# One core, two attention blocks: the fallback path moved to another DMA queue, the branch flag read earlier, the last columns in quarters

## The chip, the cores and the metric

The kernel runs on one core of a Trainium2 chip. The metric is the device time of one execution in microseconds (us). Executions of the same kernel here scatter by about 1 us in 350, so what follows leans on two things: times taken in rounds with the kernel before on the same chip, and the trace, which resolves single instructions to some nanoseconds.

## The reference, cut to what matters

Two independent problems A and B of the same shape, each a grouped-query attention block with cached K and V and an output projection; their results are placed side by side in the last axis.

```python
B, Sq, D = 16, 32, 1024;  Hq, Hkv, Sk, Dh = 32, 4, 512, 128      # all bf16
q = (x @ wq).reshape(B, Sq, Hq, Dh).transpose(0, 2, 1, 3)
scores = einsum("bhqd,bhkd->bhqk", q, repeat(k_cache, 8)) * Dh ** -0.5
o = einsum("bhqk,bhkd->bhqd", softmax(scores), repeat(v_cache, 8))
a = o.transpose(0, 2, 1, 3).reshape(B, Sq, Hq * Dh) @ wo          # and the same for B
return concatenate([a, b], axis=-1)
```

## The kernel before

The kernel has a fast path, which shifts the exponent by a constant instead of by each row's maximum, and a general path, which is slow and safe. The fast path counts how many row sums lie in a safe range; at the end every engine reads that count (the flag) and branches: if the count is full, it skips the general path. With these inputs the general path never runs. It is in the program all the same.

The parts that matter, with cuts:

```python
def general_path(tc, problems, out_flat):            # never executed here
    ...
            nc.sync.dma_start(out=x_sb[:], in_=x_v)                       # also wq, wo, outputs: all SyncE
    ...
                nc.sync.dma_start_transpose(out=kT[:], in_=k_rows[r0:r0 + HKV * SK, :])
    ...

            def f_units(pr, tt, n0, width, eng):     # output projection, one matmul per yield
                ps = psum.tile([P, NW], FP32, name="f_ps", tag="proj")
                for h in range(HQ):
                    nc.tensor.matmul(ps[:, 0:width], lhsT=oT[pr, tt][:, h, :], ...)
                    if h == HQ - 1:
                        o_sb = outp.tile([P, NW], BF16, name="o_sb")
                        if eng is nc.scalar:
                            nc.scalar.copy(out=o_sb[:, 0:width], in_=ps[:, 0:width])
                        else:
                            nc.vector.tensor_copy(out=o_sb[:, 0:width], in_=ps[:, 0:width])
                        eng.dma_start(out=out_flat[...], in_=o_sb[:, 0:width])
                    yield

            def stream():                            # the filler matmuls, in order
                ...
                for tts in ((0, 1), (2,)):
                    for nh in range(NH):
                        for tt in tts:
                            yield from f_units(1, tt, nh * NW, NW, nc.gpsimd)
                yield from f_units(1, TT - 1, 0, NW, nc.gpsimd)
                yield from f_units(1, TT - 1, NW, QW, nc.sync)            # 256 columns
                yield from f_units(1, TT - 1, NW + QW, QW, nc.scalar)     # the last 256
    ...
            nc.tensor.matmul(ok_ps[:], lhsT=cnt[:], rhs=one_col[:], start=True, stop=True)
            nc.vector.tensor_copy(out=ok_i[:], in_=ok_ps[:])
            run(units, 1 << 20)                      # all the output units that are left

    fast_path(ok_i)
    total = 2 * 2 * NG * QW
    ok = nc.values_load(ok_i[0:1, 0:1], ...)         # on every engine
    with tc.If(ok < total, preferred_fallthrough_block=True, label="general"):
        general_path(tc, problems, out_flat)
```

DMAs of the hardware queues (issued by SyncE and ScalarE) signal eight semaphores in turn, a ring, so the semaphore that the last output signals depends on how many such DMAs came before it (in the traces: numbers 101 and 103 to 109 in turn; the last output signals the first of them, 101, in the kernel before and the last, 109, in the changed one). Where the branch is skipped, each engine still has to bring the semaphores that the skipped code would have raised to the values that later code expects; for those of DMAs, the engine that would have issued them does it (in the trace of the kernel before, SyncE's eight events on the branch's line each wait for one semaphore and raise it).

Of the kernel before, what the change touches and what calls it, by code (L numbers as in the profile page):

```python
# [8 lines left out]
BF16 = mybir.dt.bfloat16  # L9
# [7 lines left out]
P = 128  # L17
HQ = 32
DH = 128
HKV = 4  # L20
# [10 lines left out]
def general_path(tc, problems, out_flat):  # L31

    nc = tc.nc
# [4 lines left out]
    KC = SK // P  # L38
# [4 lines left out]
    with ExitStack() as ctx:  # L43
# [10 lines left out]
        for x, k_cache, v_cache, wq, wo, col_off in problems:  # L54
            x_v = x.flatten_outer_dims().rearrange("(t p) d -> p t d", p=P)
            x_sb = wpool.tile([P, TT, D], BF16, name="g_x", tag="g_w")
            nc.sync.dma_start(out=x_sb[:], in_=x_v)
            xT = big.tile([P, DC, NTOK], BF16, name="g_xT")
            for tt in range(TT):
                ps = psum.tile([P, DC, P], BF16, name="g_xT_ps", tag="g_t", bufs=2)  # L60
# [6 lines left out]
            wq_v = wq.rearrange("(c p) n -> p c n", p=P)  # L67
            for c in range(HQ // WH):
                wq_sb = wpool.tile([P, DC, WH * DH], BF16, name="g_wq", tag="g_w")
                nc.sync.dma_start(  # L70
                    out=wq_sb[:], in_=wq_v[:, :, c * WH * DH:(c + 1) * WH * DH]
                )
                for hl in range(WH):
                    q_ps = psum.tile([P, NTOK], FP32, name="g_q_ps", tag="g_p", bufs=2)
                    for dc in range(DC):
                        nc.tensor.matmul(
                            q_ps[:],
                            lhsT=wq_sb[:, dc, hl * DH:(hl + 1) * DH],
                            rhs=xT[:, dc, :],
                            start=(dc == 0),  # L80
                            stop=(dc == DC - 1),
                        )
                    nc.scalar.mul(
                        out=qT[:, :, c * WH + hl, :],
                        in_=q_ps[:].rearrange("p (b s) -> p b s", s=SQ),
                        mul=SCALE,
                    )
            oT = big.tile([P, HQ, NTOK], BF16, name="g_oT")
            k_rows = k_cache.rearrange("b g k d -> (b g k) d")
            for b in range(B):  # L90
                kT = kvpool.tile([P, HKV, SK], BF16, name="g_kT")
                r0 = b * HKV * SK
                nc.sync.dma_start_transpose(out=kT[:], in_=k_rows[r0:r0 + HKV * SK, :])
                v_sb = kvpool.tile([P, HKV, KC, DH], BF16, name="g_v")
                nc.sync.dma_start(
                    out=v_sb[:], in_=v_cache[b].rearrange("g (c p) d -> p g c d", p=P)
                )
                for g in range(HKV):
                    s_ps = psum.tile([P, 2, SK], FP32, name="g_s_ps", tag="g_s")
                    for half in range(2):  # L100
                        h0 = g * REP + half * HALF
                        nc.tensor.matmul(
                            s_ps[:, half, :],
                            lhsT=qT[:, b, h0:h0 + HALF, :].rearrange("p h s -> p (h s)"),
                            rhs=kT[:, g, :],
                            start=True,
                            stop=True,
                        )
                    nmx = work.tile([P, 2], FP32, name="g_nmx")
                    nc.vector.tensor_reduce(  # L110
                        out=nmx[:], in_=s_ps[:], axis=AX.X, op=ALU.max, negate=True
                    )
                    p_sb = work.tile([P, 2, SK], BF16, name="g_p_sb")
                    rs = work.tile([P, 2], FP32, name="g_rs")
                    rr = work.tile([P, 2], FP32, name="g_rr")
                    for half in range(2):
                        nc.scalar.activation(
                            out=p_sb[:, half, :], in_=s_ps[:, half, :], func=ACTF.Exp,
                            bias=nmx[:, half:half + 1], scale=1.0,
                            accum_out=rs[:, half:half + 1],  # L120
                        )
                    nc.vector.reciprocal(out=rr[:], in_=rs[:])
                    for half in range(2):
                        nc.vector.tensor_scalar_mul(
                            out=p_sb[:, half, :], in0=p_sb[:, half, :],
                            scalar1=rr[:, half:half + 1],
                        )
                    pT_ps = psum.tile([P, KC, 2 * P], BF16, name="g_pT_ps", tag="g_t", bufs=2)
                    for half in range(2):
                        for kc in range(KC):  # L130
                            nc.tensor.transpose(
                                pT_ps[:, kc, half * P:(half + 1) * P],
                                p_sb[:, half, kc * P:(kc + 1) * P],
                                ident[:],
                            )
                    pT = work.tile([P, KC, 2 * P], BF16, name="g_pT")
                    nc.vector.tensor_copy(out=pT[:], in_=pT_ps[:])
                    o_ps = psum.tile([P, 2 * P], FP32, name="g_o_ps", tag="g_p", bufs=2)
                    for kc in range(KC):
                        nc.tensor.matmul(  # L140
                            o_ps[:],
                            lhsT=v_sb[:, g, kc, :],
                            rhs=pT[:, kc, :],
                            start=(kc == 0),
                            stop=(kc == KC - 1),
                        )
                    nc.scalar.copy(
                        out=oT[:, g * REP:(g + 1) * REP, b * SQ:(b + 1) * SQ],
                        in_=o_ps[:].rearrange("p (h s) -> p h s", s=SQ),
                    )  # L150
            wo_v = wo.rearrange("(h p) n -> p h n", p=P)
            for oc in range(NOUT // OCW):
                wo_sb = wpool.tile([P, HQ, OCW], BF16, name="g_wo", tag="g_w")
                nc.sync.dma_start(out=wo_sb[:], in_=wo_v[:, :, oc * OCW:(oc + 1) * OCW])
                for tt in range(TT):
                    f_ps = psum.tile([P, OCW], FP32, name="g_f_ps", tag="g_p", bufs=2)
                    for h in range(HQ):
                        nc.tensor.matmul(
                            f_ps[:],
                            lhsT=oT[:, h, tt * P:(tt + 1) * P],  # L160
                            rhs=wo_sb[:, h, :],
                            start=(h == 0),
                            stop=(h == HQ - 1),
                        )
                    o_sb = work.tile([P, OCW], BF16, name="g_o_sb")
                    nc.vector.tensor_copy(out=o_sb[:], in_=f_ps[:])
                    c0 = col_off + oc * OCW
                    nc.sync.dma_start(
                        out=out_flat[tt * P:(tt + 1) * P, c0:c0 + OCW], in_=o_sb[:]
                    )  # L170

# [2 lines left out]
def kernel(  # L174
# [35 lines left out]
    def fast_path(ok_i):  # L210
        with ExitStack() as fctx:
# [139 lines left out]
            def run(units, n):  # L351
                for _ in range(n):
                    next(units, None)
# [190 lines left out]
            def stream():  # L544
                for h in range(2, HQ):
                    yield from q_units(0, h)
                for h in range(HQ):
                    yield from q_units(1, h)
                for nh in range(NH):
                    for tt in range(TT):  # L550
                        yield from f_units(0, tt, nh * NW, NW, nc.gpsimd)
                for tts in ((0, 1), (2,)):
                    for nh in range(NH):
                        for tt in tts:
                            yield from f_units(1, tt, nh * NW, NW, nc.gpsimd)
                yield from f_units(1, TT - 1, 0, NW, nc.gpsimd)
                yield from f_units(1, TT - 1, NW, QW, nc.sync)
                yield from f_units(1, TT - 1, NW + QW, QW, nc.scalar)

            units = stream()  # L560
            run(units, (REP - 2) * DC + 4)
# [56 lines left out]
            for k, (lim, op) in enumerate(((1.0 / SUM_HI, ALU.is_ge), (1.0 / SUM_LO, ALU.is_le))):  # L618
# [7 lines left out]
            ok_ps = psum.tile([1, 1], FP32, name="ok_ps", tag="s")  # L626
            nc.tensor.matmul(ok_ps[:], lhsT=cnt[:], rhs=one_col[:], start=True, stop=True)  # L627
            nc.vector.tensor_copy(out=ok_i[:], in_=ok_ps[:])
            run(units, 1 << 20)

    flag = ctx.enter_context(tc.tile_pool(name="flag", bufs=1))
    ok_i = flag.tile([1, 1], I32, name="ok_i")
    fast_path(ok_i)
    total = 2 * 2 * NG * QW
    ok = nc.values_load(ok_i[0:1, 0:1], min_val=0, max_val=total,
                        skip_runtime_bounds_check_because="only compared")
    with tc.If(ok < total, preferred_fallthrough_block=True, label="general"):
        general_path(tc, problems, out_flat)

# [29 lines left out]
```

## Time and profile before

| | before |
|---|---|
| time, median of the first three runs | 350.49 us (349.77 to 350.71) |
| span of the profiled run | 348.6 us |
| TensorE busy | 342.2 us, 98% |
| last ScalarE cast to the end of the span | 4.27 us |

From the page of the kernel before, its first line, the busy line and the chain that ended last:

```profile
span 348.6 us, 5527 instructions
...
PE 342.2 (98%) x2217; PEld 221.2 (63%) x2217; DVE 282.6 (81%) x420; ACT 180.4 (52%) x197; POOL 8.9 (3%) x21
...
PE 96%; DMA 2%; SPq 1%; DVE 1%; issue 0%; ACT 0%
```

The windows view of the kernel before gives, for each stretch of the span, its length and then the busy time of each engine in it, the granted clock (PEclk), the DMA share and the DMA rate:

```profile
core 0: us, PE busy (x) PEld busy (x) DVE busy (x) ACT busy (x) POOL busy (x), PEclk, DMA share, GB/s
...
11.00:179.00 168.00, 168.00 (x1072) 107.89 (x1069) 138.03 (x197) 108.53 (x130) 0.00 (x0) 1.00 1.06 256
179.00:327.00 148.00, 147.93 (x956) 96.50 (x955) 136.10 (x201) 67.90 (x61) 7.15 (x13) 1.00 0.70 173
327.00:345.00 18.00, 17.34 (x115) 10.79 (x113) 5.16 (x11) 0.37 (x1) 1.08 (x2) 1.00 0.06 21
345.00:349.00 4.00, 0.00 (x0) 0.00 (x0) 0.00 (x0) 0.00 (x0) 0.00 (x0) 1.00 0.06 18
```

TensorE is full from 11 to 327 us, so in that stretch nothing is to be won by moving other work. Only the end is open. From the timeline of the kernel before (start, duration, engine, line, what it does):

```profile
344.07 0.27 PE L331 MATMUL f_ps<-wo_sb,oT 128*128 128x256 bf16 x1
344.38 0.37 ACT L341 CAST o_sb<-f_ps 128x256 bf16<-128x256 f32 x1 [22.13 <-PE f_ps L331]
344.78 0.38 ACTq L345 DMA_DIRECT2D out_dram<-o_sb  x1
```

The list of DMA issues says how long that last output takes to land, from its issue to the last update of its semaphore (the last figure, in us):

```profile
out_dram<-o_sb ACTq DMA_DIRECT2D x1, 64.0 KB, 1.6
```

What comes after it does not count as busy, but the profile lists it by source line. L637 is the branch, L664 the end of the kernel. A row gives the sequencer, the instruction, how many, the durations in ns, and when the first and the last of them began:

```profile
L637 SPq EVENT_SEMAPHORE  x8: 17/17/17, 346.4 to 347.0; - x8
...
L637 PEldq COMPARE_BRANCH  x1: 376/376/376, 342.8 to 342.8; - x1
...
L637 ACTq COMPARE_BRANCH  x1: 79/79/79, 345.8 to 345.8; - x1
```

```profile
L664 SPq EVENT_SEMAPHORE  x14: 17/28/28, 347.0 to 348.6; - x14
...
L664 SPq DRAIN  x3: 7/7/13, 347.8 to 348.1; - x3
```

So when the last output has landed (346.42), SyncE goes through 8 events of the skipped branch, then the 12 of the end list, and only at 347.77 executes its first DRAIN, from which the closing barriers begin: 1.35 us for 20 events.

### The profile page before, as it was taken

How to read it: one execution, taken by the hardware profiler on the slowest of the kernel's cores; microseconds unless marked ns; L12 is line 12 of the kernel's file. 1: busy time of each engine (PE TensorE's matmuls, PEld its weight loads, DVE VectorE, ACT ScalarE, POOL GpSimd, SP SyncE). 2: the span in 40 equal slices, each digit the busy share in tenths (PEclk: the TensorE clock that was granted, in tenths of full speed). 3: DMA queues.
4: the chain of work that ended last, by engine and by line, in shares of the span. 5: the costliest groups of instructions: out<-in, count | busy, mean ns of one | idle time of the engine just before them, and what ended most of it. 6: DMA issues, size and time to landing. Idle time of an engine off the chain costs nothing.

```text
span 348.6 us, 5527 instructions
## 1 busy us (share of the span) xinstructions
PE 342.2 (98%) x2217; PEld 221.2 (63%) x2217; DVE 282.6 (81%) x420; ACT 180.4 (52%) x197; POOL 8.9 (3%) x21
## 2 busy tenths in 40 slices
PE   7999999999999999999999999999999999999995
PEld 4556666666666666666666666666666666666554
DVE  2118988888988889898889989999999999899710
ACT  3347667666666766666654454454455445445000
POOL 0000000000000000000000000000000000000010
PEclk9999999999999999999999999999999999999999
DMA  7999999899997899999999459995589995400000
GB/s 224 240 302 333 168 253 270 241 276 256 270 253 197 172 249 222 311 267 268 279 316 222 115 124 270 349 212 121 137 259 263 252 227 102 120 18 0 15 32 20
DMA packets 125069, 71.70 MB, mean 206 GB/s; under 512 B 73616, under 2 KB 124048, under 8 KB 125040
## 3 DMA queue, kind: packets, MB, share of 16 engines
q1 hardware_dynamic: 124176, 69.29, 81.7%
q0 software_dynamic: 720, 1.97, 1.7%
q8 instruction: 18, 0.29, 0.3%
q14 instruction: 11, 0.09, 0.1%
q10 hardware_dynamic: 144, 0.07, 0.1%
HBM read 51.38 MB, written 2.10 MB: 153 GB/s over the span
## 4 chain that ended last, share of the span: by engine, by line
PE 96%; DMA 2%; SPq 1%; DVE 1%; issue 0%; ACT 0%
PE f_ps L331 32%; PE q_ps L312 31%; PE ob L431 16%; PE s_ps L371 16%; DMA x_sb<-in_A_x_dram 2%; PE q_ps L516 1%; SPq L468 0%; DVE parts L390 0%; PE sums L407 0%; SPq L471 0%; DVE o_sb L343 0%; PE xT_ps L506 0%; ACT o_sb L341 0%; DVE cs L399 0%; PE ok_ps L627 0%
## 5 line engine op out<-in xcount | busy, mean ns | idle before, releaser
L379 ACT ACTIVATE p_sb<-s_ps,shift 128x1024 bf16<-128x1024 f32 x128 | 142.5, 1113 | 113.1 <-PE s_ps L371 100.4
L390 DVE TRANSPOSE_TENSOR_REDUCE parts<-p_sb 128x32 f32<-128x1024 bf16 x128 | 158.2, 1236 | 22.1 <-ACT p_sb L379 21.6
L331 PE MATMUL f_ps<-wo_sb,oT 128*128 128x512 bf16 (+1 forms) x544 | 133.3, 367 | 0.0
L312 PE MATMUL q_ps<-xT,wq_sb 128*128 128x512 bf16 x496 | 129.6, 380 | 0.0
L371 PE MATMUL s_ps<-qT,kT 128*128 128x256 bf16 x512 | 76.8, 273 | 0.0
L431 PE MATMUL ob<-p_sb,v_sb 128*128 128x256 bf16 x512 | 76.8, 273 | 0.0
L331 PEld LDWEIGHTS <-oT 128*128 128x128 bf16 x544 | 53.0, 98 | 33.8
L312 PEld LDWEIGHTS <-wq_sb 128*128 128x128 bf16 x496 | 48.4, 98 | 34.7 <-DMA wq_sb<-in_A_wq_dram 0.3
L371 PEld LDWEIGHTS <-kT 128*128 128x128 bf16 x512 | 56.9, 113 | 20.9
L431 PEld LDWEIGHTS <-v_sb 128*128 128x128 bf16 x512 | 50.1, 98 | 19.8 <-DVE oT L453 0.2
L453 DVE TENSOR_TENSOR oT<-r,ob 128x512 bf16<-128x512 f32 x64 | 43.9, 685 | 12.8 <-PE ob L431 9.4
L418 DVE STREAM_TRANSPOSE r<-rall 128x512 f32<-128x512 f32 x64 | 45.5, 711 | 2.2
L320 ACT CAST qT<-q_ps 128x512 bf16<-128x512 f32 x62 | 36.1, 583 | 21.3 <-PE q_ps L312 19.2
L407 PE MATMUL sums<-cs,fold 128*128 128x16 f32 x64 | 22.9, 357 | 0.1
L343 DVE CAST o_sb<-f_ps 128x512 bf16<-128x512 f32 (+1 forms) x16 | 10.8, 673 | 10.8 <-PE f_ps L331 10.0
L399 DVE TENSOR_REDUCE cs<-parts 128x16 fp32r<-128x64 f32 x64 | 16.8, 262 | 2.2
L407 PEld LDWEIGHTS sums<-cs,fold 128*128 128x128 f32 x64 | 12.1, 190 | 8.3 <-DVE cs L399 0.9
L345 POOL DMA_DIRECT2D out_dram<-o_sb x15 | 8.2, 549 | 329.3 <-DVE o_sb L343 298.6
L416 DVE RECIPROCAL rall<-sums 128x16 f32<-128x16 f32 x64 | 14.1, 220 | 0.0
L341 ACT CAST o_sb<-f_ps 128x256 bf16<-128x256 f32 x1 | 0.4, 372 | 22.1 <-PE f_ps L331 22.1
L509 DVE COPY xT<-xT_ps 128x512 bf16<-128x512 bf16 x4 | 1.7, 424 | 5.6 <-PE xT_ps L506 5.6
L509 ACT COPY xT<-xT_ps 128x512 bf16<-128x512 bf16 x4 | 2.3, 585 | 5.7 <-PE xT_ps L506 5.7
(27 smaller groups left out, 24.1 us busy)
## 6 DMA issues: line engine op xcount, KB each, us to landing
v_sb<-in_A_v_cache_dram SPq DMA_DIRECT2D x16, 512.0 KB, 5.0
wq_sb<-in_B_wq_dram SPq DMA_DIRECT2D x8, 1024.0 KB, 6.5
wo_sb<-in_A_wo_dram SPq DMA_DIRECT2D x8, 1024.0 KB, 7.6
v_sb<-in_B_v_cache_dram SPq DMA_DIRECT2D x16, 512.0 KB, 4.5
wo_sb<-in_B_wo_dram SPq DMA_DIRECT2D x8, 1024.0 KB, 8.8
wq_sb<-in_A_wq_dram SPq DMA_DIRECT2D x7, 1024.0 KB, 7.4
out_dram<-o_sb POOLq DMA_DIRECT2D x15, 128.0 KB, 3.6
x_sb<-in_A_x_dram SPq DMA_DIRECT2D x4, 256.0 KB, 3.9
```

What stands on the lines that cost most here:

```text
L312: nc.tensor.matmul(ps[:], lhsT=w[:, dc, (h % 4) * DH:(h % 4 + 1) * DH], rhs=xT[pr][:, dc, :], start=(dc == 0), stop=(dc == DC - 1),)
L320: nc.scalar.copy(out=qT[pr, g][:, :, hl, :], in_=ps[:].rearrange("p (b s) -> p b s", s=SQ),)
L331: nc.tensor.matmul(ps[:, 0:width], lhsT=oT[pr, tt][:, h, :], rhs=wo_tiles[pr, nh, h // REP][:, h % REP, off:off + width], start=(h == 0), ...
L371: nc.tensor.matmul(s_ps[:, c, :], lhsT=kT[:, i % GRP, c, :], rhs=qT[pr, g][:, b, :, :].rearrange("p h s -> p (h s)"), start=True, stop=True,)
L379: nc.scalar.activation(out=p_sb[:], in_=s_ps[:], func=ACTF.Exp, bias=shift[:], scale=SCALE)
L390: nc.vector.tensor_reduce(out=parts[j][:, q, :, :].rearrange("p c h -> p (c h)"), in_=st[i]["p"][:].rearrange("p c (h s) -> p (c h) s", s=SQ),
L399: nc.vector.tensor_reduce(out=cs[:], in_=parts.pop(j)[:].rearrange("p q c h -> p q h c"), axis=AX.X, op=ALU.add,)
L407: nc.tensor.matmul(sums[:], lhsT=fold[:].rearrange("p r s -> p (r s)"), rhs=cs[:].rearrange("p q h -> p (q h)"), start=True, stop=True,)
L416: nc.vector.reciprocal(out=rall[:, j, :], in_=pair.pop(j)[:])
L418: nc.vector.transpose(out=r[:].rearrange("p n s -> p (n s)"), in_=rall[:, j, :].unsqueeze(2).to_broadcast([P, 2 * REP, SQ]),)
L431: nc.tensor.matmul(ob[j][:, q, :], lhsT=v_sb[:, i % GRP, c, :], rhs=st[i]["p"][:, c, :], start=(c == 0), stop=(c == KC - 1),)
L453: nc.vector.tensor_tensor(out=out, in0=rcp.pop(j)[:].rearrange("p (q h) s -> p q h s", h=REP), in1=ob.pop(j)[:].rearrange("p q (h s) -> p ...
```

## The change

Four edits: the general path issues all its DMAs from GpSimd and transposes K on TensorE; six output DMAs of problem B move from GpSimd to SyncE; the last 256 columns become two units of 128; the flag is loaded 24 matmuls into the output matmuls that are left, rather than after all of them. The intent is a shorter end. Cut to its core:

```diff
-            nc.sync.dma_start(out=x_sb[:], in_=x_v)
+            nc.gpsimd.dma_start(out=x_sb[:], in_=x_v)
 ... (the same for wq, wo, V and the outputs of the general path)
-                nc.sync.dma_start_transpose(out=kT[:], in_=k_rows[r0:r0 + HKV * SK, :])
+                k_sb = kvpool.tile([P, HKV, KC, DH], BF16, name="g_k")
+                nc.gpsimd.dma_start(out=k_sb[:], in_=k_cache[b].rearrange(...))
+ ... (four TensorE transposes and one copy for each g)
-                            yield from f_units(1, tt, nh * NW, NW, nc.gpsimd)
+                            yield from f_units(1, tt, nh * NW, NW, nc.sync)
                 yield from f_units(1, TT - 1, 0, NW, nc.gpsimd)
                 yield from f_units(1, TT - 1, NW, QW, nc.sync)
-                yield from f_units(1, TT - 1, NW + QW, QW, nc.scalar)
+                yield from f_units(1, TT - 1, NW + QW, P, nc.sync)
+                yield from f_units(1, TT - 1, NW + QW + P, P, nc.scalar)
 ...
+            run(units, 24)
+            ok = nc.values_load(ok_i[0:1, 0:1], ...)
             run(units, 1 << 20)
```

More of the change, by code (lines that the diff above doesn't have):

```diff
@@ L69, in general_path @@
                 wq_sb = wpool.tile([P, DC, WH * DH], BF16, name="g_wq", tag="g_w")
-                nc.sync.dma_start(
+                nc.gpsimd.dma_start(
                     out=wq_sb[:], in_=wq_v[:, :, c * WH * DH:(c + 1) * WH * DH]
@@ L88, in general_path @@
             oT = big.tile([P, HQ, NTOK], BF16, name="g_oT")
-            k_rows = k_cache.rearrange("b g k d -> (b g k) d")
             for b in range(B):
-                kT = kvpool.tile([P, HKV, SK], BF16, name="g_kT")
-                r0 = b * HKV * SK
-                nc.sync.dma_start_transpose(out=kT[:], in_=k_rows[r0:r0 + HKV * SK, :])
+                k_sb = kvpool.tile([P, HKV, KC, DH], BF16, name="g_k")
+                nc.gpsimd.dma_start(
+                    out=k_sb[:], in_=k_cache[b].rearrange("g (c p) d -> p g c d", p=P)
+                )
                 v_sb = kvpool.tile([P, HKV, KC, DH], BF16, name="g_v")
-                nc.sync.dma_start(
+                nc.gpsimd.dma_start(
                     out=v_sb[:], in_=v_cache[b].rearrange("g (c p) d -> p g c d", p=P)
                 )
+                kT = kvpool.tile([P, HKV, SK], BF16, name="g_kT")
+                for g in range(HKV):
+                    kT_ps = psum.tile([P, KC, P], BF16, name="g_kT_ps", tag="g_t", bufs=2)
+                    for kc in range(KC):
+                        nc.tensor.transpose(kT_ps[:, kc, :], k_sb[:, g, kc, :], ident[:])
+                    nc.vector.tensor_copy(
+                        out=kT[:, g, :], in_=kT_ps[:].rearrange("p c k -> p (c k)")
+                    )
                 for g in range(HKV):
@@ L153, in general_path @@
                 wo_sb = wpool.tile([P, HQ, OCW], BF16, name="g_wo", tag="g_w")
-                nc.sync.dma_start(out=wo_sb[:], in_=wo_v[:, :, oc * OCW:(oc + 1) * OCW])
+                nc.gpsimd.dma_start(out=wo_sb[:], in_=wo_v[:, :, oc * OCW:(oc + 1) * OCW])
                 for tt in range(TT):
@@ L167, in general_path @@
                     c0 = col_off + oc * OCW
-                    nc.sync.dma_start(
+                    nc.gpsimd.dma_start(
                         out=out_flat[tt * P:(tt + 1) * P, c0:c0 + OCW], in_=o_sb[:]
@@ L628, in fast_path @@
             nc.vector.tensor_copy(out=ok_i[:], in_=ok_ps[:])
+            run(units, 24)
+            ok = nc.values_load(ok_i[0:1, 0:1], min_val=0, max_val=total,
+                                skip_runtime_bounds_check_because="only compared")
             run(units, 1 << 20)
+            return ok
     flag = ctx.enter_context(tc.tile_pool(name="flag", bufs=1))
     ok_i = flag.tile([1, 1], I32, name="ok_i")
-    fast_path(ok_i)
     total = 2 * 2 * NG * QW
-    ok = nc.values_load(ok_i[0:1, 0:1], min_val=0, max_val=total,
-                        skip_runtime_bounds_check_because="only compared")
+    ok = fast_path(ok_i)
     with tc.If(ok < total, preferred_fallthrough_block=True, label="general"):
```

## The prediction

> **What bounds the kernel now.** TensorE. The page gives PE 342.2 of 348.6 us; the chain that ended last is 96% PE. In the windows view PE is busy 168.00 of 168 us from 11 to 179 us and 147.93 of 148 from 179 to 327, at full granted clock. So only the tail after the last matmul (about 344.34 us) is open: 4.3 us.
>
> **The tail (timeline; sequencer rows of the branch's line and the last line).** Last matmul, ScalarE cast 344.38 (0.37 us), ScalarE issues the last output at 344.78, which lands after 1.6 us, at 346.42, when SyncE's first semaphore event runs. Then SyncE alone executes 8 events of the skipped branch (346.4 to 347.0: it raises each of its DMA semaphores, because the general path uses them) and 12 end-of-kernel events (to 347.7), one every 0.066 us. The first drain is at 347.77, the closing barriers 0.88 us more.
>
> **The change.**
> 1. General path on GpSimd's queue. Never executed, but the skipped branch no longer has semaphores of SyncE to raise: those 8 events vanish. GpSimd's new waits are on transfers long landed. The last output's semaphore now also comes last in SyncE's end list (built program). From landing to the first drain: 1.35 us becomes one wait, 0.07. Saves 1.3 us, all on the critical path.
> 2. Flag loaded early. A load costs 0.48 to 0.54 us per sequencer. In before, ScalarE's runs in the shadow of the final landing: its drain is at 346.3, just before 346.42. TensorE's load begins with 17 matmuls still to start, so it runs ahead of the array; 0.5 us mid-stream is covered (the Trainium skill, "TensorE: Matmul & The Clock Gate", Architectural detail, gives a 64-deep queue; 17 pairs are 34 instructions, so this trace shows at least that). Worth about 0 alone.
> 3. Quarters: 32 matmuls of 256 columns, 109.3 ns apart, become 64 of 128. The trace's own 128-column matmuls with weight loads start 56 ns apart (the same page, Back-to-back issue gap, says about 81 sustained; the trace is used): 3.58 against 3.50 us, +0.08, minus 0.05 for the shorter last matmul. The ScalarE cast shrinks from 0.37 to about 0.27 (estimate from 512 columns 0.58, 256 columns 0.37). Net -0.07 us; the 32 KB landing stays near 1.6.
> 4. Six B outputs move from GpSimd to SyncE. Their casts are ready while SyncE waits for buffers, so K/V loads slip by at most an issue (0.4 us) against microseconds of slack. 0 us.
>
> Sum: -1.3 to -1.4 us. Predicted 349.1 us, 80% range 348.4 to 350.0. Chances: faster by over 2%: 1%; within 2%: 98%; slower: 1%.
>
> **What would show it.** Step 1: SyncE's branch line has no semaphore events; landing to first drain about 0.1 us. Step 2: no gap of PE near 337 us. Step 3: last-unit matmuls 56 ns apart, last cast about 0.27 us at about 344.4. Step 4: windows from 179 to 327 us still full PE. Span 347.2 to 347.4.
>
> **What would make it wrong.** TensorE's queue running dry after its flag load (up to +0.6 us); 128-column pairs at 66 to 81 ns (+0.7 to +1.7 us); narrow 256-byte rows landing more slowly; ScalarE or GpSimd arriving after the landing (the jump over the now larger branch; ScalarE took 0.42 us after its compare); a SyncE output wait holding back a V load; scatter (0.9 us between three runs before).

## The result, and the profile after

Beside the kernel before, the changed kernel took 349.5 us (median of 4, 349.34 to 349.55) against 350.51 (4 runs). Ratios here are the mean time of one kernel's runs over that of the other's of the same rounds, with the first run of each set (the profiled one) left out, so not quite the ratio of the quoted medians: 0.9976, 95% interval 0.9961 to 0.9990, or -0.84 us. A second set of rounds with the unaltered changed kernel (after_again, below) gave 0.9966 (0.9953 to 0.9980), or -1.19 us.

The page of the changed kernel:

```profile
span 347.7 us, 5593 instructions
...
PE 342.7 (99%) x2249; PEld 221.7 (64%) x2249; DVE 283.0 (81%) x421; ACT 180.5 (52%) x197; POOL 5.7 (2%) x15
...
PE 96%; DMA 2%; SPq 1%; DVE 1%; issue 0%; ACT 0%
```

Its windows: the middle is as full as it was, so no output on SyncE's queue held back a load that TensorE waited for.

```profile
11.00:179.00 168.00, 168.00 (x1072) 107.89 (x1070) 138.06 (x197) 108.64 (x130) 0.00 (x0) 1.00 1.04 257
179.00:327.00 148.00, 147.94 (x955) 96.41 (x954) 136.22 (x201) 67.96 (x61) 4.46 (x8) 1.00 0.67 172
```

Its timeline at the end, and the landing in its list of issues:

```profile
344.56 0.27 ACT L349 CAST o_sb<-f_ps 128x128 bf16<-128x128 f32 x1 [22.21 <-PE f_ps L339]
344.86 0.38 ACTq L353 DMA_DIRECT2D out_dram<-o_sb  x1
```

```profile
out_dram<-o_sb ACTq DMA_DIRECT2D x1, 32.0 KB, 1.9
```

The branch (L648) and the end of the kernel (L675). SyncE has no event at the branch any more, and its end list starts at 343.7, before the last output is even issued:

```profile
L648 PEldq COMPARE_BRANCH  x1: 397/397/397, 343.4 to 343.4; - x1
L648 SPq COMPARE_BRANCH  x1: 68/68/68, 343.5 to 343.5; - x1
```

```profile
L675 SPq EVENT_SEMAPHORE  x14: 17/28/28, 343.7 to 347.7; - x14
...
L675 SPq DRAIN  x3: 7/7/13, 346.8 to 347.1; - x3
```

The difference of the two spans (-0.93 us) adds up from the two traces:

| from the trace, us | before | after | difference |
|---|---|---|---|
| start to first exponential (start-up) | 23.19 | 23.30 | +0.11 |
| first to last exponential | 297.94 | 297.94 | 0.00 |
| last exponential to last cast (TensorE's last units) | 23.25 | 23.33 | +0.08 |
| last cast to issue of the last output | 0.40 | 0.30 | -0.10 |
| issue to landing, as SyncE sees it | 1.64 | 1.90 | **+0.26** |
| landing to SyncE's first drain | 1.35 (20 events) | 0.07 (1 event) | -1.29 |
| drain to the end of the span | 0.88 | 0.90 | +0.02 |

The second row, 297.93 or 297.94 us in all fourteen traces, is the whole pipelined part; the first ranges from 22.71 to 23.92 us and seems to be noise of the first loads. Spans are therefore best compared from the last cast on.

Two terms call for an explanation: is the -1.29 the work of the fallback path alone, as the prediction had it, and why does a smaller output land later?

### The profile page after: what moved, and what is told of

The parts are those of the page before. It is cut to its first block, busy times and chain, and to the rows that moved or that the text cites. A ratio compares the mean times of both kernels' runs of the same rounds, so it can differ in the third digit from the quotient of the medians.

```text
span 347.7 us, 5593 instructions
## 1 busy us (share of the span) xinstructions
PE 342.7 (99%) x2249; PEld 221.7 (64%) x2249; DVE 283.0 (81%) x421; ACT 180.5 (52%) x197; POOL 5.7 (2%) x15
## 4 chain that ended last, share of the span: by engine, by line
PE 96%; DMA 2%; SPq 1%; DVE 1%; issue 0%; ACT 0%
PE f_ps L339 32%; PE q_ps L320 31%; PE ob L439 16%; PE s_ps L379 16%; DMA x_sb<-in_A_x_dram 2%; PE q_ps L524 1%; SPq L476 0%; DVE parts L398 0%; PE sums L415 0%; SPq L479 0%; DVE o_sb L351 0%; PE xT_ps L514 0%; DVE cs L407 0%; ACT o_sb L349 0%; PE ok_ps L636 0%
## 5 line engine op out<-in xcount | busy, mean ns | idle before, releaser
L339 PE MATMUL f_ps<-wo_sb,oT 128*128 128x512 bf16 (+2 forms) x576 | 133.3, 356 | 0.0
L351 DVE CAST o_sb<-f_ps 128x512 bf16<-128x512 f32 (+2 forms) x17 | 11.1, 650 | 12.2 <-PE f_ps L339 11.4
L353 POOL DMA_DIRECT2D out_dram<-o_sb x9 | 5.0, 556 | 332.6 <-DVE o_sb L351 312.1
```

What stands on the lines that cost most here:

```text
L339: nc.tensor.matmul(ps[:, 0:width], lhsT=oT[pr, tt][:, h, :], rhs=wo_tiles[pr, nh, h // REP][:, h % REP, off:off + width], start=(h == 0), ...
```

## The experiments

Theories. **E**: what the end costs is the number of SyncE's semaphore events left after the last landing. That depends on the branch's events (edit 1) and also on which semaphore of the ring the last output signals, which the moved outputs and the quarters shift by adding hardware DMAs (six and one). Rivals: the fallback path alone brings all of it (R1); the flag loads do (R2). **F**: the landing is late because an instruction block that TensorE fetches around its branch comes over the same DMA engines just then. Rival **L**: rows of 256 bytes land later than rows of 512.

All kernels gave correct results. Each was timed in 5 rounds against the kernel before.

| kernel | time against before, us (ratio, interval) | events after landing, us to drain | landing, us | last cast to end, us |
|---|---|---|---|---|
| before | | 20, 1.350 | 1.64 | 4.27 |
| only_general | -0.63 (0.9982, 0.9968 to 0.9995) | 8, 0.489 | 1.65 | 3.43 |
| only_sync_out | -0.39 (0.9989, 0.9975 to 1.0003) | 14, 0.874 | 1.65 | 3.80 |
| only_quarters | +1.02 (1.0029, 1.0016 to 1.0043) | 19, 1.240 | 2.39 | 4.81 |
| only_flag | +0.35 (1.0010, 0.9996 to 1.0024) | 20, 1.345 | 1.63 | 4.26 |
| after / after_again | -0.84 / -1.19 | 1, 0.065 | 1.90 / 1.79 | 3.16 / 3.04 |
| no_quarters | -1.54 (0.9956, 0.9943 to 0.9970) | 2, 0.126 | 1.64 | 3.07 |
| merged_last | -0.81 (0.9977, 0.9964 to 0.9991) | 2, 0.127 | 1.69 | 3.01 |
| halves_two_dmas | -0.81 (0.9977, 0.9963 to 0.9990) | 1, 0.065 | 1.58 | 3.37 |
| no_general | -0.53 (0.9985, 0.9972 to 0.9999) | 13, 0.807 | 1.86 | 3.84 |
| no_sync_out | -0.60 (0.9983, 0.9969 to 0.9997) | 7, 0.428 | 1.85 | 3.47 |
| no_flag | -0.35 (0.9990, 0.9976 to 1.0004) | 1, 0.065 | 2.41 | 3.67 |
| halves_split_cast | -0.88 (0.9975, 0.9961 to 0.9988) | 1, 0.065 | 2.28 | 3.53 |

The times in us are the ratio's distance from 1, times about 350.5. The last three columns are from the profiled run of each. The "only" kernels are the kernel before with one edit, the "no" kernels the changed kernel with one edit undone. Kernels with 128-column units have 0.08 us more of TensorE ahead of the last cast; in halves_split_cast the last cast itself begins 0.33 us later than in the kernel before.

### One edit at a time

**only_general**, the kernel before with the general path of the changed one.

> The kernel before with the general path alone taken to GpSimd's queue. Theory E (what counts is how many semaphore events SyncE still has to run after the last output lands, about 0.067 us each): 20 events in the kernel before; here the branch's 8 are gone, but the last output still signals the first of SyncE's 8 hardware DMA semaphores, so 8 of the end list's 12 remain to be run after the landing. 20 to 8: -0.8 us, from landing to first drain 0.55 us instead of 1.35. Rival R1 (my prediction's reading, the gain is all due to the skipped branch and this part alone brings it): -1.3 us, landing to drain 0.07 us. Rival R2 (the flag load is what helps): 0.

Measured: 8 events, 0.489 us to the drain, -0.63 us. R1 (-1.3) and R2 (0) lie outside the interval. The end of that kernel (its last line is L672; no event is left on its branch's line):

```profile
L672 SPq EVENT_SEMAPHORE  x14: 17/28/28, 342.8 to 348.0; - x14
...
L672 SPq DRAIN  x3: 7/7/13, 347.2 to 347.5; - x3
```

Compare the first drain with the landing of its last output, which SyncE saw at 346.72: the fallback path is worth 12 events, not all 19.

**only_sync_out**

```diff
-                            yield from f_units(1, tt, nh * NW, NW, nc.gpsimd)
+                            yield from f_units(1, tt, nh * NW, NW, nc.sync)
```

> The kernel before with only the six B outputs moved from GpSimd to SyncE. Theory E: six more hardware DMAs turn the ring of 8 semaphores on by six, so the last output signals the 7th of SyncE's list instead of the 1st; 6 of the branch's 8 events are done before it lands, 2 + 12 = 14 are left instead of 20: -0.4 us, landing to first drain 0.95 us. Prediction's step 4: 0 us. If a SyncE wait held back a V load, TensorE would show a gap between 280 and 327 us and the time would rise.

Measured: 14 events, 0.874 us. The branch's 8 events are still there, but they now begin at 342.8, well ahead of the landing, and only the last two of them come after it:

```profile
L637 SPq EVENT_SEMAPHORE  x8: 17/17/17, 342.8 to 346.5; - x8
```

The time, -0.39 us, is what E expected, but its interval still holds 0; the event times of the trace decide, not the clock. TensorE shows no gap. So an edit that takes nothing off the chain that ends last moves the end by 0.47 us (4.27 to 3.80), by turning the ring.

**only_quarters**

```diff
-                yield from f_units(1, TT - 1, NW + QW, QW, nc.scalar)
+                yield from f_units(1, TT - 1, NW + QW, P, nc.sync)
+                yield from f_units(1, TT - 1, NW + QW + P, P, nc.scalar)
```

> The kernel before with only the last columns in quarters. Theory L (rows of 256 bytes land later, 1.9 us as in the trace of after, against 1.64 us): +0.06 us of TensorE, -0.10 us of cast, +0.26 us of landing, one event fewer after it -0.07: +0.15 us. Prediction's step 3: -0.1 us with the event, last landing 1.6 us.

Measured: +1.02 us; both expectations missed. The last output landed 2.39 us after its issue, not 1.9. The DMA view of this kernel in the window from 344.5 to 346.6 us shows why. Its first row is the mean busy share of the 16 DMA engines in 40 slices, in tenths, a packet's whole time being put into the slice in which it begins; then come the queues with packets, MB and share of the 16 engines' time:

```profile
DMA  0500000000090000000000047850000110130000
...
q10 hardware_dynamic: 144, 0.03, 8.5%
q8 instruction: 1, 0.02, 3.1%
q14 instruction: 2, 0.02, 2.8%
```

q10 is ScalarE's queue, the last output. Most of its packets pass in slices 23 to 26 (345.7 to 345.9), but a thin rest, nine of the 144 packets, or one sixteenth, drags on to 346.5. q8 carried one packet of 16 KB, an instruction block, that began at 345.09 and took 1.06 us, until 346.15. The same view of the kernel before, 345.6 to 346.1 us, has one compact hump and no instruction packet beginning in it:

```profile
DMA  0000115457698899899995856443230100000000
...
q10 hardware_dynamic: 144, 0.07, 45.6%
```

**only_flag**, the kernel before with the early load of the flag.

> The kernel before with only the flag load moved among the last output units. Theory E and the prediction's step 2: 0 us within 0.15; ScalarE's drain moves to about 0.5 us before the landing but nothing waits for it; no gap of TensorE. Rival R2 (the loads at the end are on the critical path): -0.5 us.

Measured: the end is the same to 0.01 us (4.26 against 4.27), ScalarE's drain comes 0.65 us before the landing where it was 0.09, and nothing is gained. The mean time is 0.35 us above before, more than the 0.15 I allowed, with an interval that holds 0; R2's -0.5 is excluded. The trace has no counterpart to that +0.35, so I take it for scatter.

### Why the last output lands late

That 16 KB block begins 1.13 to 1.19 us after TensorE's compare-and-branch in 13 of the 14 traces (1.42 in only_flag), while its distance from every other engine's branch varies by over 1 us. So it follows TensorE's branch. TensorE's sequencer runs ahead of the array by a number of instructions, not by a time: the flag load, where it is late, and the branch, where the load is early, began with 17 matmuls still to start in all fourteen traces. That is 1.85 us at 109 ns each in the kernel before, and 0.95 us at the 56 ns of 128 columns. So quarters bring the branch, and the block, later against the last output. The Trainium skill, "Runtime: NRT & Kernel Launch", Instruction fetch mechanics, says that sequencers fetch their instructions in blocks over a DMA queue of their own and that a taken branch breaks the sequential prefetch; "DMA: Bandwidth & Descriptors", Issuing engines are not separate DMA queues, says that DMAs run on the same 16 DMA engines whether ScalarE, SyncE or GpSimd starts them; it does not speak of instruction blocks there. The packets here agree: the blocks come on queues of their own (q8, q14), TensorE's after its branch.

The packed traces also list the 16 updates by which the last output's semaphore is raised. In the kernel before, all 16 come within 0.13 us (346.28 to 346.41). In the changed kernel fifteen have come by 346.35 and the last comes at 346.74; in only_quarters fifteen by 346.45 and the last at 347.20. So the output is not slow as a whole: one sixteenth of it is late. That is what one occupied DMA engine of the 16 would give; which engine carried which packet is not in the traces kept.

**no_quarters** (the last unit 256 columns again), **merged_last** (quarters, but the two casts into one tile and one DMA of 256 columns, so 512-byte rows), **halves_two_dmas** (256-column unit, one cast, sent as two DMAs of 256-byte rows) and **after_again** (unaltered).

```diff
# halves_two_dmas, beside undoing the quarters
-                        eng.dma_start(out=out_flat[..., c0:c0 + width], in_=o_sb[:, 0:width])
+                        step = P if eng is nc.scalar else width
+                        for w0 in range(0, width, step):
+                            eng.dma_start(out=out_flat[..., c0 + w0:c0 + w0 + step], in_=o_sb[:, w0:w0 + step])
# merged_last: the first quarter casts into o_sb[:, 0:128] and sends nothing,
# the second casts into o_sb[:, 128:256] and sends both
```

> The changed kernel with the last columns back in halves of 256. Theory F: the last output lands late where a 16 KB instruction block that TensorE fetches after its branch is still coming in over a shared DMA engine when the output's packets start; 128-column matmuls shorten the lead of TensorE's sequencer over the array, so the branch and its fetch come later relative to the last matmul. Here the lead is back to 1.85 us: the fetch ends over 0.5 us before the first packet, landing 1.64 us, 2 events after it. Against the changed kernel of these rounds: -0.05 TensorE, +0.10 cast, -0.25 landing, +0.07 event: -0.15 us; against before -1.15 us. Theory L (256-byte rows land late) expects the same of this run. Prediction's step 3: +0.1 us against the changed kernel.

Measured: landing 1.64 us, 2 events, as expected. L expected the same, so the run does not choose between F and L. The time, -1.54 us, is the best of all, but against after_again of the same rounds (-1.19) the intervals overlap, and with the first runs counted the two are at -1.37 and -1.26.

> The changed kernel, its last two quarters still computed and cast apart but sent in one DMA of 256 columns, so rows are 512 bytes and matmuls still 128 columns. Theory F: TensorE's branch is as late as in the changed kernel, so the landing stays at 1.9 us or more (1.8 to 2.4). Theory L: rows of 512 bytes again, landing 1.64 us, -0.2 us of time against the changed kernel.

Measured: 1.69 us, between the two expectations, so alone it tells little: F's lower bound of 1.8 was missed.

> The changed kernel with halves of 256 columns, one cast of the last one, but its output sent in two DMAs of 128 columns, 256-byte rows, from ScalarE. Theory F: TensorE's branch is early, so the second DMA lands 1.64 us (1.55 to 1.75) after its issue; the time is about 0.4 us above the halves for the second issue. Theory L: 256-byte rows, landing 1.9 us or more.

Measured: the second DMA of 256-byte rows landed in 1.58 us. From the DMA view of that kernel, 345.9 to 346.8 us (the list holds the issue that falls in the window, in us to landing):

```profile
out_dram<-o_sb ACTq DMA_DIRECT2D x1, 32.0 KB, 1.6
```

Rows of 256 bytes are not slow by themselves. L falls as the cause.

> The changed kernel unaltered, as the control of these rounds. Theory E and F: -0.9 us against before, 1 event after the landing, landing late at 1.8 to 2.4 us with the block fetch ending within 0.2 us of the first packet of the last output, or after it.

Measured: landing 1.79, block ending 0.16 us before the first packet. The landing is slightly under the 1.8 that I gave.

Put in order of the time from the end of the 16 KB block to the first packet of the last output, the traces line up (a negative number: the block ended after it):

| kernel | block end to first packet, us | landing, us |
|---|---|---|
| no_flag | -0.46 | 2.41 |
| only_quarters | -0.44 | 2.39 |
| after | +0.05 | 1.90 |
| no_general | +0.08 | 1.86 |
| no_sync_out | +0.09 | 1.85 |
| after_again | +0.16 | 1.79 |
| merged_last | +0.25 | 1.69 |
| only_sync_out | +0.33 | 1.65 |
| before, only_general | +0.75, +0.74 | 1.64, 1.65 |
| only_flag, no_quarters, halves_two_dmas | +1.05, +1.33, +1.78 | 1.63, 1.64, 1.58 |

One trace is left out: halves_split_cast has +1.52 and 2.28 us, so TensorE's block cannot be its cause (see below). The order as a whole was seen after the runs. Of the runs for which F gave both numbers beforehand, no_quarters and no_flag met them, after_again missed the landing by 0.01 us, and no_flag is the one that F alone expected to be later. merged_last, which missed, fits the order: its gap was 0.25. Why a block that ended up to 0.25 us before still delays the output is not shown; the traces give only when packets began and how long they took.

### One edit undone

**no_general**: the changed kernel with the general path of the kernel before.

> The changed kernel with the general path back on SyncE's queue and its DMA transposes. Theory E: the last output signals the 8th of SyncE's semaphores, so only one of the branch's 8 events is left after the landing, but all 12 of the end list follow: 13 events, landing to first drain 0.87 us instead of 0.07, time about -0.2 us against before (the changed kernel had -0.8 and -1.2 in two sets of rounds). Rival R3 (only the branch's own events count): 1 event after the landing, time as the changed kernel, -1.0.

Measured: 13 events, 0.807 us to the drain, -0.53 us. R3's -1.0 is just outside the interval (0.9972 is -0.98 us), E's -0.2 inside; the 13 events, which E gave beforehand against R3's 1, decide. Here the branch's events are nearly all done before the landing, and the end list alone costs 0.74 us more than in the changed kernel.

**no_sync_out**: the changed kernel with the six outputs on GpSimd.

> The changed kernel with the six B outputs back on GpSimd. Theory E: the ring of semaphores stands at the 2nd, so 7 events of the end list follow the landing: landing to first drain 0.43 us, time about 0.4 us above the changed kernel, -0.6 us against before. Prediction's step 4: moving the outputs is worth 0, so -1.0. Landing as in the changed kernel, 1.8 to 1.9 us.

Measured: 7 events, 0.428 us, -0.60 us; landing 1.85. The interval holds -1.0, so again it is the trace that refutes "worth 0".

**no_flag**: the changed kernel with the flag load at the end.

> The changed kernel with the flag load back at the end of each engine's stream. Theory F: TensorE's 0.49 us load and then its branch come about 0.55 us later relative to the last matmul, so its 16 KB block fetch runs into the last output's packets as in the kernel with the quarters alone: fetch ending over 0.3 us after the first packet, landing 2.2 us or more, time 0.4 to 0.6 us above the changed kernel, -0.5 us against before. Prediction's step 2: the early load is worth 0, landing as in the changed kernel, -1.0 us.

Measured: TensorE's branch at 344.4, block until 346.65, first packet of the output at 346.19, landing 2.41 us, -0.35 us. Both numbers of F's expectation (block ending over 0.3 us after the first packet, landing 2.2 us or more) are met, with rows and matmuls as in the changed kernel, and step 2's -1.0 is excluded. Its branch and its packets from 344.5 to 347.1 us:

```profile
L646 PEldq COMPARE_BRANCH  x1: 393/393/393, 344.4 to 344.4; - x1
```

```profile
DMA  6200000040000000900000000059510000002000
...
q8 instruction: 1, 0.02, 2.5%
```

The same view of the changed kernel, 344.5 to 346.6 us: the block begins in the first slice, the output's packets pass in one hump.

```profile
DMA  9000000000000000000000016973100000060000
...
q8 instruction: 1, 0.02, 3.4%
```

So the early load, worth nothing alone, is worth 0.5 to 0.6 us together with the quarters in the traces (last cast to end 3.67 against 3.16 and 3.04; by the clock the intervals still overlap): without it, TensorE's 0.49 us load stands ahead of the branch just where the lead is short.

**halves_split_cast**: meant to beat both.

```diff
# beside undoing the quarters
-                yield from f_units(1, TT - 1, 0, NW, nc.gpsimd)
+                yield from f_units(1, TT - 1, 0, NW, nc.sync)
 ...
-                            nc.scalar.copy(out=o_sb[:, 0:width], in_=ps[:, 0:width])
+                            half = width // 2
+                            nc.vector.tensor_copy(out=o_sb[:, 0:half], in_=ps[:, 0:half])
+                            nc.scalar.copy(out=o_sb[:, half:width], in_=ps[:, half:width])
```

> A version meant to beat both: the changed kernel with halves instead of quarters, one more output on SyncE so that the last output again signals the last semaphore of the list (1 event), and the last 256 columns cast half by VectorE and half by ScalarE. Theory E and F: branch early, landing 1.64 us, 1 event, last cast to issue 0.30 us instead of 0.40: -0.2 to -0.3 us against the changed kernel, -1.2 to -1.4 us against before. If the two casts do not overlap, no gain over the plain halves.

In the trace both hopes failed. (By the clock, -0.88 us, its interval reaches from -0.42 to -1.37 and still holds the -1.2 that was expected; the profiled run, at 350.82 us, was the slowest of its five.) The built program makes the ScalarE cast wait for the VectorE one, so they ran one after the other and ScalarE's began 0.33 us later than in the kernel before: the timeline names VectorE's cast as the releaser.

```profile
345.38 0.27 ACT L351 CAST o_sb<-f_ps 128x128 bf16<-128x128 f32 x1 [22.46 <-DVE o_sb L350]
```

And the landing was 2.28 us although TensorE's block ended 1.52 us before. Two 8 KB instruction blocks of another queue began at 346.57 and 347.16 while the output's packets ran from 346.55 to 347.27, and VectorE, with its cast now last, had branched only at 345.07, where it had branched at 342.79 in the changed kernel. Again one of the 16 updates was late: fifteen had come by 347.34, the last came at 347.94. That fits F carried over to another engine's block, but no run takes it apart.

## Why the prediction was right or wrong

The predicted 349.1 us (348.4 to 350.0) holds the measured 349.5, and "within 2%" was right. The mechanism, SyncE's list after the last landing, was right too. The saving was over-sized, though: -1.3 to -1.4 us predicted, -0.84 and -1.19 measured. The range would have held a saving of 0.5 us as well (350.49 less 350.0), so the hit says little of the sum. Point by point:

- **What bounds it.** Right: the middle is 297.94 us in every trace, and only the end moved.
- **Step 1, 1.35 us of events to 0.07.** The size for the whole change was right (1.350 to 0.065). The attribution was not: the fallback path alone leaves 8 events and brings 0.86 of it in the trace, 0.63 us by the clock. The rest comes from the place in the ring. The prediction noted that the last output's semaphore "now also comes last", but did not see that the moved outputs and the quarters put it there. That the sum of step 1 came out right is owed to all four edits being made together.
- **Step 2, the early flag load, "worth about 0 alone".** True alone (4.26 against 4.27 us). But beside the quarters it is worth 0.5 to 0.6 us in the traces, since it takes a load out of TensorE's shortened lead. No queue ran dry: TensorE shows no gap.
- **Step 3, "net -0.07 us; the 32 KB landing stays near 1.6".** This is the step that failed. Its +0.08 for TensorE (56 ns a matmul) and -0.10 for the cast were met. The further -0.05 for the shorter last matmul was not: from the last exponential to the last cast the traces give +0.08 in all. And the landing was 1.90 and 1.79 us: that +0.15 to +0.26 us is the mis-sized term. The step came to +0.13 to +0.24 us in place of -0.07. From the last cast on, with TensorE's 0.08, the traces give -1.03 and -1.14 us for the whole change, against -0.84 and -1.19 by the clock. The list of risks had "narrow 256-byte rows landing more slowly"; halves_two_dmas refuted that cause, and no_flag, with the order of the 16 KB blocks, showed another: the block that TensorE fetches after its branch. How a block that has already ended still delays the output stays open.
- **Step 4, the six outputs, "0 us".** Nothing was held back, as predicted, yet the step is worth 0.36 us in the changed kernel's trace (0.428 to 0.065), through the ring alone.

By the traces the quarters do not pay: last cast to end plus the 0.08 us of TensorE is 3.24 and 3.12 us with them and 3.07 without. no_quarters beats the kernel before by 1.54 us. Whether it beats the changed kernel is open: 0.9956 and 0.9966 have overlapping intervals.

## What to carry to other kernels

When the bound engine is full and only the end is left, look past the busy rows: count the semaphore events that still run after the last landing, about 0.065 us each here, and see which edits decide their number (every count of events that E gave beforehand was met), including the code that never runs and the mere count of DMAs. A branch costs more than its compare: TensorE's instruction block began 1.13 to 1.42 us after its branch and took about a microsecond more, and where it met the last output, that landed late. Here the output was on time with TensorE's branch 1.95 us or more ahead of the output's issue (halves_split_cast excepted), 0.05 to 0.26 us late at 1.48 us, and 0.75 to 0.77 us late at 0.89 us. And where edits interact, run each alone and each undone: in the traces the early flag load was worth nothing alone and half a microsecond in company.

## What the Trainium skill lacked or had wrong

- "TensorE: Matmul & The Clock Gate", Back-to-back issue gap, gives about 81 ns sustained for a 128-column matmul with its weight load, and about 56 ns only for what it calls an isolated one. Here such pairs start 56 ns apart (64 in a row in the changed kernel), and 256-column ones 109 ns apart.
- "Advanced Engine Details and Errata", Control Flow Timing, gives about 108 ns for a compare-and-branch. Here it took 59 to 89 ns on four sequencers and 376 to 402 ns on TensorE's.
- "Runtime: NRT & Kernel Launch", Instruction fetch mechanics, speaks of 16 KiB blocks. Here one instruction queue carried 16 KB packets and another 8 KB ones, and the page does not say that a block can delay a data transfer: 16 KB took 0.95 to 1.35 us at the end, and the last output landed up to 0.77 us later when it overlapped one.
- I found no page that says that the ring position of the last DMA's semaphore matters: 0.47 us between the kernel before and only_sync_out, at 0.061 to 0.068 us for each event (8 in 0.489 us, 20 in 1.350 us).
